# Splitting the merge's products between even and odd steps of a chunked delta-rule attention

## The chip, the cores and the metric

One core of a Trainium2 chip runs the whole program in one launch. The metric is the device time of an execution in microseconds, the median of three runs. Its engines are named as the profile does: PE is TensorE's matmuls, PEld its weight loads, DVE VectorE, ACT ScalarE, POOL GpSimd, SP SyncE, which issues the loads.

## The reference

A delta-rule attention of 4 batches x 8 heads, 768 tokens, head size 48, is followed by two MLP-like stages: a 2-D Fourier transform along tokens and channels with an MLP behind it, then a gated MLP whose gate is mixed along the tokens. The change touches only the attention:

```python
k_n = k / (np.linalg.norm(k, axis=-1, keepdims=True) + 1e-06)
state = np.zeros((B, H, D, D))
for t in range(S):
    kt, vt, bt = k_n[:, :, t], v[:, :, t], beta[:, :, t, None]
    y[:, :, t] = np.einsum('bhd,bhde->bhe', q[:, :, t], state)
    v_old = np.einsum('bhde,bhd->bhe', state, kt)
    state = state + bt[..., None] * np.einsum('bhd,bhe->bhde', kt, vt - v_old)
```

All is float32.

## The kernel before

**Chunks.** The 768 tokens are cut into 12 chunks of 64; with 4 batches that makes 48 units of work, which the code calls chunks and numbers bc = 0 to 47 in the order of a skewed list (`SEQ`). One chunk holds all 8 heads of its batch. In a chunk the recurrence becomes a triangular system of 64 x 64 per head: T, the inverse of a unit lower triangular matrix, is applied to the scaled keys and values, and the state is carried from chunk to chunk.

**Solver.** T is made for 8 chunks at a time (a block). VectorE inverts the two diagonal 32 x 32 squares of all of them together, at the end transposing them into `Tc` (line 346, two instructions); ScalarE takes the keys' norms (line 141). The solver is a generator. `Spread` advances it to a due share of its cost at fixed places of a step: `part(c1)` ahead of stage_d, `part(c2)` behind stage_a, `part(1)` at the end. A solver's steps are t = -3 to 2, 3 to 12, 13 to 20, 21 to 28 and 29 to 36 (`STARTS`).

**Loop.** `for t in range(-3, 48)` (line 631) does in each step, in this order: the scaling of chunk t + 2's values (`values`, on VectorE at line 488 for even chunks from 8 on, else on ScalarE), `part(c1)`, stage_d of chunk t (lines 533 and 534: output and new state `Sb`), stage_c of chunk t + 1 (line 513: keys times state; VectorE's `cw` at line 515) woven with stage_a of chunk t + 20 (line 220: Gram products), `part(c2)`, the diagonal of the next two chunks (`diag`), stage_b of chunk t + 2 (line 498: T times keys and values), in odd steps a `merge`, then the load of queries and `part(1)`. From t = 37 on steps are `light`: there is no solver. From t = 36 on the values of chunk t + 3 are scaled in the middle of step t (line 664), and the first products of the Fourier transform fill in behind stage_b. From then on `next(loads)` at the end of a step loads the transform's tables `sc` and `dc` (128 x 1281 and 97 x 386) and pieces of the weights, w.

**Merge.** The lower left square of T for chunks of a pair g8 comes from two rounds of products. The first: 16 products of 32 x 32 (line 467), the lower squares, `gas` times `Tc`, copied by ScalarE into `ZS` (line 471). The second: 16 products of 32 x 64 (line 469), the whole rows, `ZS` times `Tc`, copied into `TT` (line 474), which stage_b reads. Both write one PSUM bank (bankZ) at different partitions and rows. `merge(g8, first, second)` does the first for g8 and the second for g8 - 1. An odd step does both in one loop, product by product in turn, but for pairs whose first round stands at t % 8 = 5 by itself, where a new block begins.

**Loads of kv.** Keys and values of a chunk (192 KB) go into the space that the first round read (`gas`), so a load waits for the lower squares. It stands behind the merge of the odd step, two chunks at a time (lines 678 and 679).

**What sets the order.** Each engine takes its instructions in the order in which the code emits them: `chain()` at the end of each step ties every instruction to the one before it on its engine. SyncE's queue is filled in that order too.

Of the kernel before, what the change touches and what calls it, by code (L numbers as in the profile page):

```python
# [23 lines left out]
NBC = B * NC  # L24
# [42 lines left out]
class Kernel:  # L67
# [36 lines left out]
    def load(self, out, in_):  # L104
        return self.nc.sync.dma_start(out=out, in_=in_)
# [13 lines left out]
    def attention(self, cp, pg, pe, p, x, filler, after_solves):  # L119
# [115 lines left out]
        def mask_q(bc):  # L235

            out = gas[bc // 4 * 4, 4][:, bc % 4 : bc % 4 + 2, :, :C]
            first, second = (SEQ[i][1] < HALF for i in (bc, bc + 1))
            if first == second:
                m = mask_a(bc, C).unsqueeze(1)  # L240
            else:
                m = mk[:, : 4 * C].rearrange("p (a c) -> p a c", a=2)[:, :, :C]
                m = (m[:, ::-1] if first else m).unsqueeze(2)
            nc.vector.tensor_tensor(out=out, in0=out, in1=m.to_broadcast([128, 2, HP, C]), op=MUL)
# [202 lines left out]
        light = lambda t: t >= 8 * NB - 11  # L447

        def diag(g8):

            o = (g8 % 4) * 8
            for h, us in enumerate(up):
                (nc.vector.tensor_copy if light(2 * g8 - 3) else nc.scalar.copy)(
                    out=TT[g8 % NTT][us, :, C * h + 32 : C * h + C], in_=Tts[g8 // 4][us, o : o + 8]
                )

        def merge(g8, first, second):

            z0, z1 = zz[:, g8 % 2 * 256 : g8 % 2 * 256 + 256].rearrange("p (g n) -> p g n", g=8), zz.rearrange("p (g n) -> p g n", g=8)
            T0, o0 = (Tts[g8 // 4] if first else None), (g8 % 4) * 8  # L460
            T1, o1 = (Tts[(g8 - 1) // 4] if second else None), ((g8 - 1) % 4) * 8
            tt = TT[(g8 - 1) % NTT]
            for g in range(8):
                for h in range(2):
                    if first:
                        ga = gas[g8 * 2 + g // 4][:, g % 4]
                        nc.tensor.matmul(z0[lo[h], g], lhsT=ga[up[h], C : C + 32], rhs=T0[up[h], o0 + g], start=True, stop=True)
                    if second:
                        nc.tensor.matmul(z1[up[h], g], lhsT=T1[lo[h], o1 + g], rhs=ZS[(g8 - 1) % 2][lo[h], g], start=True, stop=True)  # L469
            if first:  # L470
                nc.scalar.mul(ZS[g8 % 2][:96, :, 32:], z0[:96], -1.0)
            if second:
                for h in range(2):
                    nc.scalar.copy(out=tt[lo[h], :, C * h : C * h + C], in_=z1[up[h]])


        def load_kv(bc):
            load(out=gas[bc][:, :, C:], in_=a["kv"][bc])

        def load_qt(bc):  # L480
            qts[bc] = p.tile([112, HP, 112], F32, name="qt", bufs=CF["qt"])
            load(out=qts[bc], in_=a["qt"][bc])

        def values(bc):
            kv = gas[bc][:, :, C:]
            if light(bc - 2) or bc >= 8 and bc % 2 == 0:
                n = n_all[:, bc * 4 : bc * 4 + 4].unsqueeze(2).to_broadcast([128, HP, D])
                nc.vector.tensor_tensor(out=kv[:, :, D:], in0=kv[:, :, D:], in1=n, op=MUL)  # L488
                return
            for hp in range(HP):  # L490
                nc.scalar.activation(kv[:, hp, D:], kv[:, hp, D:], AF.Copy, scale=n_all[:, bc * 4 + hp : bc * 4 + hp + 1])

        def stage_b(bc):
            kv = gas[bc][:, :, C:]
            tt, o = TT[(bc // 2) % NTT], (bc % 2) * 4
            pb = self.bank("pb", [128, HP, 2, D])
            for hp in range(HP):
                nc.tensor.matmul(pb[:, hp].rearrange("p t d -> p (t d)"), lhsT=tt[:, o + hp], rhs=kv[:, hp], start=True, stop=True)  # L498
            wu = WU[bc % NWU]
            nc.scalar.copy(out=wu, in_=pb.rearrange("p h t d -> p h (t d)"))  # L500
            st[bc] = [wu, None]

        def stage_c(bc):
            qt = qts.pop(bc)
            if SEQ[bc][1] == 0:
                return
            w = st[bc][0]
            cw = p.tile([112, HP, 112], F32, name="cw", bufs=2)
            pc = self.bank("pc", [128, HP, 112])
            for hp in range(HP):  # L510
                for h in hs:

                    nc.tensor.matmul(pc[h, hp], lhsT=w[h, hp, :C], rhs=gas[bc][h, hp, : C + D], start=True, stop=True)  # L513
                yield
            nc.vector.tensor_sub(cw, qt, pc[:112])  # L515
            st[bc][1] = cw
# [40 lines left out]
        for n in "kq":  # L557
            t = p.tile([128, 4, HP, GA], F32, name="gak", bufs=3).rearrange("p a b c -> p (a b c)")[:112, :2048]
# [62 lines left out]
        solver, c1, c2 = None, *CF["cuts"]  # L621
# [9 lines left out]
        for t in range(T0, NBC):  # L631
            if t in STARTS:
                if solver:
                    solver.finish()
                j, span, total = STARTS[t]
                solver, since = Spread(solve(j), total), t
            part = (lambda f: solver.upto(SECOND(t + f) if j == 1 else (t - since + f) / span)) if solver and not light(t) else (lambda f: None)
            if light(t) and solver:
                solver.finish()
                solver = None  # L640

            if 0 <= t + 2 < NBC and (not light(t) or (t + 2) % 8 == 0):
                values(t + 2)
            for bc in ahead.get(t, ()):
                mask_q(bc)
            part(c1)
            if t >= 0:
                stage_d(t)
                if SEQ[t][1] == NC - 1:
                    fill.extend(filler(SEQ[t][0]))  # L650
            new = t % 8 == 5 and t + 3 < NBC
            if new:

                merge((t + 3) // 2, True, False)
                load_kv(t + 3)
                load_kv(t + 4)
                diag((t + 3) // 2)
            corrected = stage_c(t + 1) if 0 <= t + 1 < NBC else iter(())
            if t + R + 2 < HEAD or HEAD <= t + R < NBC:
                stage_a(t + R + 2 * (t < 4), corrected)  # L660
            for _ in corrected:
                pass
            if light(t + 1) and t + 3 < NBC and (t + 3) % 8:
                values(t + 3)
            part(c2)
            odd = t % 2 and (t + 3) // 2 < NBC // 2
            if t == NBC - 12:
                solver.finish()
                loads, tail = after_solves()
            if t % 2 == 0 and t % 8 != 4 and t + 4 < NBC:  # L670
                diag((t + 4) // 2)
            if (odd or light(t + 1)) and 0 <= t + 2 < NBC:
                stage_b(t + 2)
            if odd:
                g = (t + 3) // 2
                merge(g + 1, (g + 1) % 4 > 0, True)
                if (t + 5) % 8 and t + 5 < NBC:
                    load_kv(t + 5)
                    load_kv(t + 6)
            if light(t + 1):  # L680

                for _ in range(CF["dfs"][t - (NBC - 12)]):
                    while fill and next(fill[0], 1) == 1:
                        fill.pop(0)
                for _ in range(CF["cvt"][t - (NBC - 12)]):
                    next(tail, None)
            elif not odd and 0 <= t + 2 < NBC:
                stage_b(t + 2)
            if 2 <= t + 4 < NBC:
                load_qt(t + 4)  # L690
            if t == -2:
                right(2)
                left(2)
            if t == -1:
                right(3)
            if t == 0:
                left(3)
            part(1)

            while late:  # L700
                out, m0, m1 = late.pop()
                nc.vector.tensor_tensor(out=out, in0=m0, in1=m1, op=MUL)
            self.chain()
            next(loads, None)
            if t >= NBC // 2:
                next(self.words, None)
            self.chain()
# [753 lines left out]
```

## Time and profile before

| | |
|---|---|
| Runs | 843.97, 844.51, 844.6 us; median 844.51 |
| Profiled execution | 842.8 us, span 841.0 us |
| TensorE (PE) | 807.8 us busy, 96%, 10291 matmuls |
| VectorE (DVE) | 599.6 us, 71% |
| ScalarE (ACT) | 408.9 us, 49% |
| GpSimd (POOL) | 7.6 us, 1% |
| Chain that ended last | PE 83%, DVE 11%, issue 2%, DMA 2% |
| kv loads | 48 issues, 192 KB, 3.8 us to landing |

The shares are means over stages that differ: the chain that ended last is TensorE's for most of the span, since the two MLPs behind the attention are TensorE's alone. The attention's loop is a quarter of the span. There the time of a step is read from the busy time of each engine in a stretch (windows), and from what its idle time waited for. The granted clock (PEclk) is a share of TensorE's 2.4 GHz; 0.50 is 1.2 GHz.

### The profile page before, as it was taken

The page shows a single profiled execution, that of the slowest core. Times are in us where ns is not written, and L with a number is a line of the kernel's source. Part 1 is how long each engine was busy: PE and PEld are TensorE (multiplying, and loading weights), DVE is VectorE, ACT ScalarE, POOL GpSimd, SP SyncE. Part 2 cuts the span into 40 slices and gives each one's busy share as a digit, 9 for nine tenths or more (in the row PEclk, how much of TensorE's full clock was granted, in tenths as well). Part 3 has the DMA queues.
Part 4 walks back from the last instruction along what each step waited for, and adds up shares of the span by engine and source line. Part 5 has one row for each costly group of instructions (what it writes and reads, how often), then busy time and mean ns, then how long its engine had stood idle before and what let it go on. Part 6 is the DMA issues. An engine that isn't in the chain of part 4 may idle for free.

```text
span 841.0 us, 24593 instructions
## 1 busy us (share of the span) xinstructions
PE 807.8 (96%) x10291; PEld 770.3 (92%) x10291; DVE 599.6 (71%) x1715; ACT 408.9 (49%) x1026; POOL 7.6 (1%) x60
## 2 busy tenths in 40 slices
PE   7898898889999999999999999999999999999998
PEld 7788787878988999899999999999899899899998
DVE  6988779999978995682935983345678477586663
ACT  3668868878665543232232551233452553543632
POOL 1000000000000000000000000000000000000000
PEclk9769979999999999999999999999999999999999
DMA  9634444456624200000114310112001101102001
GB/s 232 175 92 125 139 122 133 110 171 175 180 80 147 103 0 2 0 13 18 42 32 124 98 34 15 48 55 66 20 9 45 62 15 43 57 25 70 21 1 57
DMA packets 56417, 62.10 MB, mean 74 GB/s; under 512 B 31665, under 2 KB 48786, under 8 KB 56306
## 3 DMA queue, kind: packets, MB, share of 16 engines
q1 hardware_dynamic: 56162, 60.38, 24.6%
q8 instruction: 81, 1.33, 0.7%
q14 instruction: 30, 0.25, 0.1%
q10 hardware_dynamic: 144, 0.15, 0.1%
HBM read 48.12 MB, written 4.72 MB: 63 GB/s over the span
## 4 chain that ended last, share of the span: by engine, by line
PE 83%; DVE 11%; issue 2%; DMA 2%; ACT 1%; SPq 0%; ACTq 0%; DVEq 0%
PE bankX L946 17%; PE bankY L959 15%; PE bankX L1144 10%; PE bankX L1124 6%; PE bankX L1092 6%; PE bankY L1172 5%; PE bankY L498 4%; PE bankX L220 3%; PE bankY L533 2%; PE bankY L513 2%; PE bankV L959 2%; PE bankX L759 2%; PE bankY L534 2%; DVE cw L515 1%; PE bankZ L469 1%
## 5 line engine op out<-in xcount | busy, mean ns | idle before, releaser
L959 PE MATMUL bankY<-w,hx 128*128 128x384 f32 x756 | 147.2, 337 | 0.0
L946 PE MATMUL bankX<-uh,w 128*128 128x384 f32 x504 | 137.8, 340 | 0.7 <-DVE ul L868 0.7
L959 PEld LDWEIGHTS bankY<-w,hx 128*128 128x128 f32 x756 | 132.4, 188 | 0.5 <-issue 0.3
L951 DVE SCALAR_TENSOR_TENSOR hx<-bankX,hx 128x384 fp32r<-128x384 f32 x84 | 46.3, 552 | 74.4 <-ACT hx L950 71.9
L950 ACT ACTIVATE hx<-bankX 128x384 fp32r<-128x384 f32 x84 | 41.2, 490 | 109.6 <-PE bankX L946 105.2
L946 PEld LDWEIGHTS bankX<-uh,w 128*128 128x128 f32 x504 | 92.2, 188 | 1.2 <-DVE ul L868 0.9
L1144 PE MATMUL bankX<-w,A 128*128 128x384 f32 x504 | 88.8, 335 | 0.0
L1144 PEld LDWEIGHTS bankX<-w,A 128*128 128x128 f32 x504 | 87.6, 188 | 0.0
L946 PE MATMUL bankX<-ul,w 128*128 128x384 f32 x252 | 85.1, 338 | 0.0
L498 PE MATMUL bankY<-gak,TT 128*128 128x96 f32 x384 | 58.7, 299 | 5.3 <-DVE gak L488 1.9
L498 PEld LDWEIGHTS bankY<-gak,TT 128*128 128x128 f32 x384 | 50.5, 204 | 14.2 <-issue 2.8
L534 PE MATMUL bankY<-WU,gak 64*64 64x48 f32 x768 | 52.1, 231 | 0.0
L1124 PE MATMUL bankX<-xh,s 128*128 128x384 f32 x192 | 50.0, 338 | 0.0
L534 PE MATMUL bankY<-Sb,cw 48*64 48x48 f32 x704 | 47.5, 226 | 2.0 <-issue 2.0
L1133 ACT CAST u<-hx 128x384 fp32r<-128x384 f32 x32 | 15.8, 513 | 67.6 <-DVE hx L1131 67.6
L220 PE MATMUL bankX<-kq 48*64 48x128 f32 x640 | 48.0, 298 | 0.5 <-issue 0.5
L946 PEld LDWEIGHTS bankX<-ul,w 128*128 128x128 f32 x252 | 47.4, 188 | 0.0
L533 PE MATMUL bankY<-Sb,cw 48*48 48x48 f32 x640 | 38.8, 211 | 8.8 <-DVE cw L515 6.4
L513 PE MATMUL bankY<-gak,WU 64*64 64x112 f32 x704 | 46.0, 270 | 1.3 <-issue 1.3
L1092 PE MATMUL bankX<-s,xh 128*128 128x512 f32 x144 | 45.9, 395 | 0.0
L533 PE MATMUL bankY<-WU,gak 64*64 64x48 f32 x704 | 44.9, 232 | 0.6 <-ACT gak L200 0.6
L533 PEld LDWEIGHTS bankY<-WU,gak 64*64 64x64 f32 x704 | 37.5, 141 | 4.9 <-issue 1.0
(240 smaller groups left out, 1846.9 us busy)
## 6 DMA issues: line engine op xcount, KB each, us to landing
qt<-in_qt_dram SPq DMA_DIRECT2D x48, 196.0 KB, 3.4
gak<-in_kv_dram SPq DMA_DIRECT2D x48, 192.0 KB, 3.8
w<-in_w_dram SPq DMA_DIRECT2D x24, 384.0 KB, 5.6
kq<-in_kc_dram SPq DMA_DIRECT2D x20, 448.0 KB, 4.1
out_dram<-x SPq DMA_DIRECT2D x24, 192.0 KB, 1.9
x<-x SPq DMA_DIRECT2D x96, 36.0 KB, 1.9
s<-in_wi_dram SPq DMA_DIRECT2D x6, 512.0 KB, 4.3
un<-xh SPq DMA_DIRECT2D x80, 36.0 KB, 1.9
```

What stands on the lines that cost most here:

```text
L220: nc.tensor.matmul(pa[q, hp], lhsT=kq[r, hp, C:], rhs=kq[r, hp], start=True, stop=True)
L498: nc.tensor.matmul(pb[:, hp].rearrange("p t d -> p (t d)"), lhsT=tt[:, o + hp], rhs=kv[:, hp], start=True, stop=True)
L513: nc.tensor.matmul(pc[h, hp], lhsT=w[h, hp, :C], rhs=gas[bc][h, hp, : C + D], start=True, stop=True)
L533: nc.tensor.matmul(ps[C * i : C * i + n - C, hp], lhsT=k[:, C:n], rhs=u, start=not last, stop=end)
L534: nc.tensor.matmul(po[hs[1 - i], hp], lhsT=k[:, :C], rhs=u, start=not last, stop=end)
L946: nc.tensor.matmul(ph, lhsT=w1[f][i][:, c * 128 : c * 128 + 128], rhs=cur[k][:, c], start=(c + j == 0), stop=(c == 2 and j == 2))
L951: nc.vector.scalar_tensor_tensor(out=hl, in0=ph, scalar=0.0, in1=hh.bitcast(F32), op0=MAX, op1=SUB)
L959: nc.tensor.matmul(acc[t], lhsT=hx[i][:, t * 128 : t * 128 + 128], rhs=w2[e][k], start=(e == 0 and j == 0), stop=(e == 11 and j == 2),)
L1092: nc.tensor.matmul(pv, lhsT=xT[t][i][:, c, kk * 128 : kk * 128 + 128], rhs=wi[2 * c + 1][k], start=(c + j == 0), stop=(c == 2 and j == 2))
L1124: nc.tensor.matmul(pu, lhsT=wi[2 * c][i][:, f * 128 : f * 128 + 128], rhs=xT[hf][k][:, c], start=(c + j == 0), stop=(c == 2 and j == 2))
L1144: nc.tensor.matmul(acc, lhsT=A[:, m, o, i, kk], rhs=Bo[name, kk][:, k], start=(kk + j == 0), stop=(kk == 2 and j == 2))
L1172: nc.tensor.matmul(po, lhsT=a[:, :128], rhs=wo[f][k], start=(f + j == 0), stop=(f == last and j == 2))
```

## The change

The merge's two rounds part. An odd step does the second alone (`merge(g + 1, False, True)`); the first moves to the even step behind it, behind stage_b (in light steps behind the transform's products), for t % 8 other than 4. The loads of kv for two chunks move with it, so they are issued one step later. The values of the even chunks that VectorE scales (`sooner`: chunks 8 and up, not those of bc % 8 = 0, nor light ones) are scaled at the end of the odd step instead of the start of the next. And `part(c1)` is left out in a solver's last step (t = 12, 20, 28 and 36), so what it would have emitted there comes with `part(c2)` and `part(1)`.

```diff
--- before.py
+++ after.py
@@ -490,6 +490,9 @@
             for hp in range(HP):
                 nc.scalar.activation(kv[:, hp, D:], kv[:, hp, D:], AF.Copy, scale=n_all[:, bc * 4 + hp : bc * 4 + hp + 1])
 
+        def sooner(bc):
+            return 8 <= bc < NBC and bc % 8 in (2, 4, 6) and not light(bc - 2)
+
         def stage_b(bc):
             kv = gas[bc][:, :, C:]
             tt, o = TT[(bc // 2) % NTT], (bc % 2) * 4
@@ -639,11 +642,12 @@
                 solver.finish()
                 solver = None
 
-            if 0 <= t + 2 < NBC and (not light(t) or (t + 2) % 8 == 0):
+            if 0 <= t + 2 < NBC and (not light(t) or (t + 2) % 8 == 0) and not sooner(t + 2):
                 values(t + 2)
             for bc in ahead.get(t, ()):
                 mask_q(bc)
-            part(c1)
+            if t - since < span - 1:
+                part(c1)
             if t >= 0:
                 stage_d(t)
                 if SEQ[t][1] == NC - 1:
@@ -673,10 +677,7 @@
                 stage_b(t + 2)
             if odd:
                 g = (t + 3) // 2
-                merge(g + 1, (g + 1) % 4 > 0, True)
-                if (t + 5) % 8 and t + 5 < NBC:
-                    load_kv(t + 5)
-                    load_kv(t + 6)
+                merge(g + 1, False, True)
             if light(t + 1):
 
                 for _ in range(CF["dfs"][t - (NBC - 12)]):
@@ -686,6 +687,10 @@
                     next(tail, None)
             elif not odd and 0 <= t + 2 < NBC:
                 stage_b(t + 2)
+            if t % 2 == 0 and t % 8 != 4 and t + 4 < NBC:
+                merge((t + 4) // 2, True, False)
+                load_kv(t + 4)
+                load_kv(t + 5)
             if 2 <= t + 4 < NBC:
                 load_qt(t + 4)
             if t == -2:
@@ -700,6 +705,8 @@
             while late:
                 out, m0, m1 = late.pop()
                 nc.vector.tensor_tensor(out=out, in0=m0, in1=m1, op=MUL)
+            if sooner(t + 3):
+                values(t + 3)
             self.chain()
             next(loads, None)
             if t >= NBC // 2:
```

TensorE at steps 22 and 23 before: L498 (stage_b) ends the even step, L533 and L534 are stage_d of the next; `WU`, `TT`, `ZS` and `Tc` are the tiles named above.

```order
L513 MATMUL bankY<-gak,WU_92 64x112 x2
L498 MATMUL bankY<-gak,TT_89 128x96 x4
L533 MATMUL bankY<-WU_92,gak 64x48
L534 MATMUL bankY<-WU_92,gak 64x48
...
L498 MATMUL bankY<-gak,TT_89 128x96 x4
L467 MATMUL bankZ<-Tc,gak 32x32
L469 MATMUL bankZ<-ZS_85,Tc 32x64
L467 MATMUL bankZ<-Tc,gak 32x32
```

The same places in the changed kernel, where stage_b is L501 and stage_d L536 and L537:

```order
L516 MATMUL bankY<-gak,WU_92 64x112 x2
L501 MATMUL bankY<-gak,TT_89 128x96 x4
L467 MATMUL bankZ<-Tc,gak 32x32 x16
L536 MATMUL bankY<-WU_92,gak 64x48
...
L501 MATMUL bankY<-gak,TT_89 128x96 x4
L469 MATMUL bankZ<-ZS_85,Tc 32x64 x16
L536 MATMUL bankY<-WU_91,gak 64x48
```

The 16 lower squares of the odd step's mixture now stand between the even step's stage_b and the next stage_d.

VectorE at step 12 before: the values of chunk 14 (L488; `n_all` are the norms), the solver's two transposes into `Tc`, then `cw` of chunk 13, between masks of the Gram products.

```order
L702 TENSOR_TENSOR gak<-bankX,mk 128x4x64
L488 TENSOR_TENSOR gak<-gak,n_all 128x4x48
L346 STREAM_TRANSPOSE Tc<-Ts 128x16x32 x2
L515 TENSOR_TENSOR cw<-qt,bankY 112x448
L702 TENSOR_TENSOR gak<-bankX,mk 128x4x64
```

And in the changed kernel:

```order
L707 TENSOR_TENSOR gak<-bankX,mk 128x4x64
L488 TENSOR_TENSOR gak<-gak,n_all 128x4x48
L518 TENSOR_TENSOR cw<-qt,bankY 112x448
L346 STREAM_TRANSPOSE Tc<-Ts 128x16x32 x2
L707 TENSOR_TENSOR gak<-bankX,mk 128x4x64
```

`cw` has come ahead of both transposes; the values stand where they stood.

SyncE's queue at steps 36 to 39 before: the tables `sc` and `dc`, the kv of chunks 40 to 43 (four) between them, and weight pieces w.

```order
L105 DMA s_4902<-in_sc_dram 128x1281
L105 DMA gak<-in_kv_dram 128x4x96 x4
L105 DMA qt<-in_qt_dram 112x448
L105 DMA s_4903<-in_dc_dram 97x386
L105 DMA w_3_5056<-in_w_dram 128x768
L105 DMA qt<-in_qt_dram 112x448
L105 DMA w_5_5130<-in_w_dram 128x768
L105 DMA gak<-in_kv_dram 128x4x96 x2
```

And in the changed kernel:

```order
L105 DMA s_4902<-in_sc_dram 128x1281
L105 DMA gak<-in_kv_dram 128x4x96 x2
L105 DMA qt<-in_qt_dram 112x448
L105 DMA s_4903<-in_dc_dram 97x386
L105 DMA w_3_5037<-in_w_dram 128x768
L105 DMA gak<-in_kv_dram 128x4x96 x2
L105 DMA qt<-in_qt_dram 112x448
```

The kv of chunks 42 and 43, the last two of the four, have come behind `dc` and a weight piece.

## Rows read from the trace of the kernel before

**Rows 1.** Windows: stretch, us; busy us (count) PE, PEld, DVE, ACT, POOL; clock; DMA; GB/s.

```profile
56.00:111.50 55.50, 49.13 (x1616) 43.80 (x1615) 43.70 (x136) 44.86 (x140) 1.70 (x19) 0.96 0.45 128
111.50:122.00 10.50, 10.26 (x234) 9.44 (x238) 6.30 (x34) 5.45 (x17) 0.16 (x1) 0.51 0.38 105
122.00:207.00 85.00, 75.45 (x2543) 67.29 (x2535) 81.93 (x306) 69.11 (x205) 1.85 (x20) 1.00 0.53 147
207.00:262.00 55.00, 52.20 (x1418) 47.32 (x1413) 46.17 (x124) 34.38 (x91) 0.00 (x0) 0.97 0.38 110
```

**Rows 2.** TensorE's waits, 124 to 207 us: line, waited for: us, times, longest.

```profile
PE bankY L533 <- DVE cw L515: 3.0, 5, 1.0
...
PE bankY L498 <- DVE gak L488: 1.9, 2, 1.2
```

**Rows 3.** TensorE's waits, 56 to 111.5 us.

```profile
PE bankY L533 <- ACT gak L200: 0.6, 1, 0.6
```

**Rows 4.** Windows: the loop's start, and the stretch ahead of the fall.

```profile
36.00:57.00 21.00, 20.85 (x456) 18.61 (x453) 20.66 (x80) 13.99 (x44) 0.00 (x0) 0.50 0.44 123
...
108.14:111.55 3.41, 1.93 (x40) 1.50 (x30) 3.38 (x7) 2.42 (x9) 0.77 (x9) 1.00 0.19 66
```

**Rows 5.** Windows, bankZ alone (no POOL column): squares, whole rows, both mixed.

```profile
76.00:78.00 2.00, 0.69 (x32) 0.58 (x32) 0.00 (x0) 0.00 (x0) 1.00 0.03 8
...
144.00:146.00 2.00, 1.08 (x32) 0.92 (x32) 0.00 (x0) 0.18 (x1) 1.00 0.24 53
...
153.00:155.50 2.50, 1.10 (x64) 0.94 (x64) 0.00 (x0) 0.65 (x2) 1.00 0.50 119
```

**Rows 6.** The chain near 113 us: start us, us, what (count).

```profile
113.49 0.99 PE bankZ L467 x32
```

**Rows 7.** Timeline, steps 8 and 9: start us, us, engine line op [idle before <-releaser].

```profile
93.05 1.13 PE L498 MATMUL bankY<-gak,TT 128*128 128x96 f32 x8
...
98.62 0.35 DVE L488 TENSOR_TENSOR gak<-gak,n_all 128x192 f32<-128x192 f32 x1
```

**Rows 8.** DMA issues, 216 to 219.3 us: count, KB each, us to landing.

```profile
gak<-in_kv_dram SPq DMA_DIRECT2D x2, 192.0 KB, 4.0
```

**Rows 9.** Timeline, steps 38 to 41, stage_b, values, stage_d.

```profile
221.60 1.24 PE L498 MATMUL bankY<-gak,TT 128*128 128x96 f32 x8
...
226.06 0.35 DVE L488 TENSOR_TENSOR gak<-gak,n_all 128x192 f32<-128x192 f32 x1
...
232.08 0.25 PE L533 MATMUL bankY<-WU,gak 64*64 64x48 f32 x1
```

**Rows 10.** SyncE's timeline (its DMA queue), 216 to 231 us.

```profile
216.58 4.57 SPq L105 DMA_DIRECT2D gak<-in_kv_dram  x4
...
221.86 0.33 SPq L105 DMA_DIRECT2D s<-in_dc_dram  x1
...
226.26 1.24 SPq L105 DMA_DIRECT2D gak<-in_kv_dram  x2
...
230.96 0.31 SPq L105 DMA_DIRECT2D qt<-in_qt_dram  x1
```

**Rows 11.** DMA issues, 225 to 228 us.

```profile
gak<-in_kv_dram SPq DMA_DIRECT2D x2, 192.0 KB, 8.1
```

**Rows 12.** SyncE's waits, 229 to 236 us.

```profile
SPq L105 <- DMA s<-in_dc_dram: 0.5, 1, 0.5
```

**Rows 13.** Timeline, step 12, 108.8 to 111.7 us.

```profile
108.81 0.23 ACT L141 ACTIVATE n<-sq 128x32 f32<-128x32 f32 x1 [0.87 <-DVE sq L262]
...
109.03 0.35 DVE L488 TENSOR_TENSOR gak<-gak,n_all 128x192 f32<-128x192 f32 x1
...
109.29 1.95 DVE L346 STREAM_TRANSPOSE Tc<-Ts 128x512 f32<-128x512 f32 x2
...
109.63 1.10 PE L498 MATMUL bankY<-gak,TT 128*128 128x96 f32 x8 [0.92 <-ACT Sb L542]
...
111.10 0.59 DVE L515 TENSOR_TENSOR cw<-qt,bankY 112x448 f32<-112x448 f32 x1
```

## Prediction

> **What bounds the kernel now.** I read the stretches of the attention stage first, since the change touches only the loop over steps t = -3 to 47, which fills about 36 to 262 us of the 841.0 us span. From 56 to 111.5 us TensorE, VectorE and ScalarE are busy for 49.1, 43.8 and 44.9 of 55.5 us (in the profile's windows PE, DVE and ACT): TensorE leads and no engine is full. From 122 to 207 us VectorE is busy for 81.9 of 85 us and TensorE for 75.5; from 207 us on TensorE for 52.2 of 55 [rows 1]. So more work for TensorE should cost most before 111 us and after 207 us, and least between. Next the waits: from 124 to 207 us TensorE loses 3.0 us at line 533 to VectorE's cw (5 waits) and 1.9 us at line 498 to the scaled values [rows 2]. Before 111.5 us one wait of 0.6 us, for ScalarE, is of that kind [rows 3]. Third, the granted clock: full before, 0.51 from 111.5 to 122 us [rows 1], and what came ahead of that fall was a stretch in which TensorE was busy for 1.93 of 3.41 us [rows 4]. The loop's first 21 us run at 0.50 as well [rows 4].
>
> **The change part by part.**
>
> *The split merge.* The odd step's merge had 16 products of the lower squares (line 467), each between two of the 16 of the whole rows (line 469). Both together take 1.10 us; the whole rows alone took 1.08, the squares alone 0.69, by the windows around one merge of each kind [rows 5]: in the mixture they hide each other. So the odd step keeps its length but for 0.02 us, and each even step with squares of its own grows by 0.69 - 0.02, say 0.65 us; at the low clock squares alone take 0.99 [rows 6], say 1.0. Eighteen merges are split, at the even t from -2 to 42 without those of t % 8 = 4.
> - t = -2, 0, 2: TensorE has no wait to fill there (busy for 20.85 of 21 us [rows 4]); the clock is low for the first and about the last: 1.0 + 0.65 + 1.0 = 2.6 us.
> - t = 6, 8, 10: the squares of 6 go right ahead of step 7's stage_d, whose wait of 0.6 us [rows 3] they fill: nothing. 8 and 10 have no such wait: 1.3 us.
> - t = 14 to 34, nine merges, 5.9 us of TensorE: VectorE sets the pace [rows 1]. Four of the five cw waits stand in a stage_d right behind an even step, where the squares now go; 3.0 us in five, and at most 0.65 of each is filled, so some 2.3 us cost nothing. For the other 3.6 the bounds are 0 (VectorE has other work meanwhile) and 3.6 (stage_c, and with it cw, comes as much later); VectorE, 96% busy, speaks for the lower half, and I take 1.5.
> - t = 38, 40, 42: those of 38 come ahead of a wait, and of 42 I expect the same: nothing (0.65 each if not). Those of 40 go into the last term.
>
> *The loads of kv.* They still wait for the squares, and so are issued one step later. Up to t = 34 this just costs nothing. The shortest way is that of chunk 12: stage_b of step 8 ends at 93.05 + 1.13 = 94.2 us, its values are scaled at 98.62 [rows 7]; half the squares (0.3) and a landing of 4.0 us [rows 8] make 98.5. The end of the loop is different. There even chunks' values are scaled in the middle of odd steps (line 664): chunk 42's at 226.06 us; stage_b of step 38, behind which its load now goes, ends at 221.60 + 1.24 = 222.8 us [rows 9]. With 0.3 and 4.0 that is 227.1, 1.0 us late. But the queue ahead of it changes too. Before, kv of 42 and 43 left among the four that begin at 216.58 us, ahead of the table dc (221.86) [rows 10]; now dc and one piece of the weights go first. What was queued behind dc landed late: the kv issued at 226.26 us [rows 10] took 8.1 us [rows 11] instead of 4.0 [rows 8], to 234.4. SyncE waited for dc until 230.9 us [rows 10, 12], 9 us behind its issue. With two kv loads fewer ahead of it dc may leave some 2 us sooner and land at 228.8; by the same distance (234.4 - 230.9 = 3.5 us with two weight pieces between, here one) chunk 42's kv lands between 230 and 232, and I take 230.4. VectorE then stands for 230.4 - 226.3 = 4.1 us, and it takes its work in order: behind these values stand the sums that feed the DFT, and then cw of step 41. TensorE has to wait for them in its DFT products and starts step 41's stage_d, at 232.08 us before [rows 9], 4.1 us later, and 0.65 more for the squares of 40. From there to the loop's end TensorE is nearly full [rows 1], so nothing gives this back: 4.7 us. The bounds are 0.6 (kv is in time) and 6.5 (it lands at 232).
>
> The Trainium skill, "DMA: Bandwidth & Descriptors", section "Why a DMA increments its semaphore by 16 and not by 1", says that a DMA is spread over the largest number of engines, up to 16, that divides its slowest dimension. By that rule dc, of 97 rows, would sit on one engine, and only the part of kv on that engine would be held up; the late landings behind dc agree, though no view here shows single engines. Without it, by the landing of 4.0 us alone, the sum would be some 3 us less.
>
> *Values at the end of the odd step.* On VectorE nothing was issued between the end of a step and the start of the next, so the instruction stands where it stood. Cost 0.
>
> *part(c1) left out in a solver's last step.* It moves cw. At t = 20 and 28 cw goes ahead of the first of two transposes of Tc; what follows needs both, and their end doesn't move but by cw's 0.59 us, under VectorE's full load: 0. At t = 12 it goes ahead of both. There stage_b waited 0.92 us until 109.63 us for ScalarE's copy of Sb, and ScalarE had stood 0.87 us at line 141; then stage_d waited for cw, which stood behind two transposes of 1.95 us, until 111.7 us [rows 13]. Now line 141 comes behind ScalarE's copies, stage_b can start with the values (109.4), and cw is done by 110.0 us. Both waits go; the next is that of step 13's squares for Tc, 0.6 us later than before, at 111.9 instead of 113.4 (their start [rows 6]): 1.5 us gained. These waits are what stood ahead of the fall of the clock [rows 4]. Without them I expect no fall. What the 10.5 us at half speed can give back is bounded by VectorE, busy for 6.30 of them [rows 1]: at most 4.2 us, the 1.5 included. I take -4.2 without the fall; with it, -1.5.
>
> **Sum**, against the profiled execution's own 842.8 us (the span of 841.0 and 1.8 around it): 2.6 + 1.3 + 1.5 - 4.2 + 4.7 = +5.9, so 848.7. The median of the runs, 844.51, is 1.7 above it, so I forecast 850.4.
>
> The Trainium skill, "TensorEngine Tiling (Array Packing)", section "Key Properties", has the engine drain whenever its tiling mode changes, which speaks against splitting a group. The rows for squares and whole rows alone [rows 5] hold such a change already. By the rule as by the rows the sum stays.
>
> **Rivals.**
> 1. The clock falls at 111 us anyway. For it: step 13's squares and a wait for Tc are still there, at little work for TensorE. Against: two waits go. Then 2.6 + 1.3 + 1.5 - 1.5 + 4.7 = +8.6: 853.1.
> 2. Chunk 42's kv lands in time, since dc is the smaller part of what fills the queues there. Against: dc's 9 us. Then 4.7 becomes 0.6 and the sum +1.8: 846.3.
> 3. Faster: TensorE's extra products are hidden in every even step, because the waits behind them end on ScalarE and VectorE, whose order doesn't change. For it: VectorE's 81.9 of 85 us, and no engine full before 111 us. Against: TensorE leads there. Its place is the even steps from 8 to 34; the squares cost nothing, kv is in time, the clock doesn't fall: -4.2 + 0.6 = -3.6, 840.9. It decides if stage_d of the odd steps starts no later, behind the end of the step's chain on VectorE, than before.
> That the change doesn't do what it says holds for the values alone (above).
>
> **How the numbers follow.** Forecast 0.42, rival 1 0.20, rival 2 0.20, rival 3 0.18. A measurement of this kernel tells 0.2% from no change, which is 1.7 us: from 842.8 to 846.2 is no change. The forecast and rival 1 lie above that; rival 2 lies at its upper edge, and I count 0.05 of it as slower and 0.15 as the same; rival 3 is faster but for 0.02. Faster 0.16, same 0.17, slower 0.67. The terms' bounds (0 to 3.6, 0.6 to 6.5, -1.5 to -4.2) give the forecast its own range of 846 to 854, and rival 1 up to 856; with rival 2 and a part of rival 3 the whole range is 842 to 856.
>
> **What would show it.** In the profile after: line 467 alone with some 0.69 us at the end of even steps; less waiting at the stage_d behind them; no clock at half speed near 111 us; VectorE waiting about 4 us at line 488 for kv near the loop's end. It would be wrong if that wait is under 1 us, or if the even steps before 111 us are no longer than before.

## The result and the profile after

The changed kernel took 854.27 us (median of 8 runs, 847.76 to 856.51), the kernel before 845.61 us beside it (8 runs, 843.97 to 847.76): a ratio of 1.0089, with a 95% interval of 1.0063 to 1.0114 (the two medians alone give 1.0102). The change is slower, where 850.4 us had been forecast. Ratios and their intervals, here and below, leave out executions of more than 1.5% above the fastest of the same kernel; medians and ranges are over all. The profiled execution took 855.76 us. Its page begins so (span; busy time of each engine; granted clock in 40 slices):

```profile
span 854.0 us, 24588 instructions
...
PE 822.1 (96%) x10291; PEld 782.6 (92%) x10291; DVE 599.4 (70%) x1715; ACT 408.4 (48%) x1026; POOL 7.6 (1%) x60
...
PEclk9769999999959999999999999999999999999999
```

The work is the same; TensorE is busy for 14.3 us more. The slices place most of that: one 5 in the twelfth slice, near the loop's end, which the kernel before did not have. The windows of the same columns as [rows 1] show the stretches:

```profile
111.50:122.00 10.50, 9.01 (x284) 7.82 (x280) 10.16 (x39) 7.63 (x24) 0.93 (x10) 1.00 0.48 133
122.00:207.00 85.00, 79.35 (x2532) 70.90 (x2525) 80.54 (x304) 68.58 (x205) 1.86 (x20) 1.00 0.53 146
...
230.40:233.70 3.30, 1.46 (x10) 1.31 (x10) 2.35 (x5) 1.42 (x4) 0.00 (x0) 0.96 0.49 143
233.70:253.00 19.30, 19.30 (x216) 17.53 (x214) 6.89 (x16) 6.10 (x15) 0.00 (x0) 0.50 0.16 44
```

The low clock that [rows 1] had from 111.5 to 122 us is gone: 1.00 there, and 284 matmuls instead of 234. From 122 to 207 us TensorE works 3.9 us more and VectorE 1.4 us less. And from 233.7 to 253 us TensorE now runs at half speed, behind 3.3 us in which it was busy for 1.46.

What stands ahead of that, in the timeline of VectorE, TensorE and SyncE's queue at steps 38 to 40 (start, us, instruction, and in brackets the idle time before it and what ended it):

```profile
231.28 0.36 DVE L488 TENSOR_TENSOR gak<-gak,n_all 128x192 f32<-128x192 f32 x1 [3.95 <-DMA gak<-in_kv_dram]
```

```profile
231.90 1.10 PE L501 MATMUL bankY<-gak,TT 128*128 128x96 f32 x8 [1.54 <-DVE gak L488]
233.35 0.53 PE L760 MATMUL bankX<-s,s 128*97 128x65 f32 x2 [0.35 <-DVE s L748]
```

```profile
220.27 0.33 SPq L105 DMA_DIRECT2D s<-in_dc_dram  x1
220.65 0.69 SPq L105 DMA_DIRECT2D w<-in_w_dram  x1
224.57 1.22 SPq L105 DMA_DIRECT2D gak<-in_kv_dram  x2
```

Chunk 42's values waited 3.95 us for kv, which now leaves at 224.57 us behind dc (before: 216.58, ahead of it [rows 10]) and took 6.8 us to land (median of the two). Behind them TensorE stood for 1.54 us in stage_b and 0.35 us at the transform's products.

The squares alone in an even step, in a window of bankZ as in [rows 5], take what they were priced at:

```profile
84.50:86.00 1.50, 0.69 (x32) 0.58 (x32) 0.00 (x0) 0.08 (x1) 1.00 0.04 7
```

### The profile page after: what moved, and what is told of

It reads as the page before. It is cut to its first block, busy times and chain, and to the rows that moved or that the text cites. A ratio compares the mean times of both kernels' runs of the same rounds, so it can differ in the third digit from the quotient of the medians.

```text
span 854.0 us, 24588 instructions
## 1 busy us (share of the span) xinstructions
PE 822.1 (96%) x10291; PEld 782.6 (92%) x10291; DVE 599.4 (70%) x1715; ACT 408.4 (48%) x1026; POOL 7.6 (1%) x60
## 4 chain that ended last, share of the span: by engine, by line
PE 84%; DVE 9%; issue 2%; DMA 2%; ACT 1%; SPq 0%; ACTq 0%; DVEq 0%
PE bankX L953 17%; PE bankY L966 15%; PE bankX L1151 10%; PE bankX L1131 6%; PE bankX L1099 6%; PE bankY L1179 5%; PE bankY L501 4%; PE bankX L220 3%; PE bankX L766 2%; PE bankZ L469 2%; PE bankY L516 2%; PE bankV L966 2%; PE bankY L536 2%; PE bankY L537 2%; PE bankZ L467 1%
## 5 line engine op out<-in xcount | busy, mean ns | idle before, releaser
L501 PE MATMUL bankY<-gak,TT 128*128 128x96 f32 x384 | 57.7, 296 | 5.7 <-DVE gak L488 2.2
L501 PEld LDWEIGHTS bankY<-gak,TT 128*128 128x128 f32 x384 | 49.7, 202 | 14.4 <-issue 4.2
L537 PE MATMUL bankY<-WU,gak 64*64 64x48 f32 x768 | 50.3, 227 | 0.1
L537 PE MATMUL bankY<-Sb,cw 48*64 48x48 f32 x704 | 45.4, 222 | 0.9 <-issue 0.9
L536 PE MATMUL bankY<-WU,gak 64*64 64x48 f32 x704 | 43.1, 226 | 1.5 <-ACT WU L503 0.8
L518 DVE TENSOR_TENSOR cw<-qt,bankY 112x448 f32<-112x448 f32 x44 | 27.0, 614 | 21.3 <-PE bankX L220 10.9
L536 PEld LDWEIGHTS bankY<-WU,gak 64*64 64x64 f32 x704 | 36.7, 137 | 5.0 <-issue 1.9
```

The lines of the kernel that those rows point to most:

```text
L536: nc.tensor.matmul(ps[C * i : C * i + n - C, hp], lhsT=k[:, C:n], rhs=u, start=not last, stop=end)
L537: nc.tensor.matmul(po[hs[1 - i], hp], lhsT=k[:, :C], rhs=u, start=not last, stop=end)
```

## The experiments

Two theories stood at first. A: the loss lies at the loop's end, where kv is late because dc stands ahead of it, and the low clock follows from that wait. B: the low clock comes somewhere anyway. Since the executions of one kernel differ by several us here (the kernel before from 839.4 to 855.0 us in the 35 runs of one series), most of what follows rests on the profiles: on the time from the start of one stage_b to that of another, read from the traces. Steps -2 to 6 are the time from stage_b of step -2 to that of step 6, and so on; a star marks a part in which the clock was low (at the start every kernel has it low until 57 to 62 us, which is not marked; the two profiles in which it stayed low until 66 and 67 us are).

| Kernel | -2 to 6 | 6 to 12 | 12 to 14 | 14 to 35 | 37 to 39 | 39 to 42 |
|---|---|---|---|---|---|---|
| before | 41.37* | 26.92 | 12.75* | 87.75 | 6.88 | 16.51 |
| before, again | 39.99 | 30.86* | 8.51 | 90.14* | 6.80 | 17.06 |
| before, cw first | 40.31* | 31.55* | 7.72 | 88.00 | 7.17 | 16.51 |
| before, cw first, second series | 40.27* | 28.53 | 8.70 | 94.47* | 7.30 | 21.90* |
| before, dc ahead | 41.89* | 34.14* | 8.57 | 89.08 | 13.86* | 16.31 |
| split to 10 | 40.52 | 30.70* | 9.35 | 88.02 | 6.91 | 17.06 |
| split 14 to 34, cw first | 40.53 | 26.84 | 7.44 | 89.77* | 7.31 | 19.70* |
| changed | 40.38 | 30.26 | 8.57 | 88.94 | 7.61 | 28.62* |
| changed, again | 42.58* | 31.20* | 12.27* | 95.22* | 7.36 | 21.76* |
| changed, end joined | 40.08 | 30.22 | 9.20 | 88.67 | 6.74 | 16.41 |
| changed, dc a step later | 40.01 | 31.37* | 7.44 | 88.25 | 9.67* | 17.46* |
| changed, dc in two | 40.23 | 30.40 | 8.53 | 93.95* | 7.36 | 17.10 |
| changed, cw behind | 40.12 | 28.90 | 12.08* | 91.10* | 7.36 | 20.45 |
| changed, filled | 40.73 | 30.92 | 7.97 | 88.70 | 7.77 | 20.58 |

**The end joined.** In the changed kernel, from step 37 on:

```diff
-                merge(g + 1, False, True)
+                merge(g + 1, t >= 37 and (g + 1) % 4 > 0, True)
+                if t >= 37 and (t + 5) % 8 and t + 5 < NBC:
+                    load_kv(t + 5)
+                    load_kv(t + 6)
...
-            if t % 2 == 0 and t % 8 != 4 and t + 4 < NBC:
+            if t % 2 == 0 and t % 8 != 4 and t + 4 < 42:
```

> The changed kernel, but from step 37 on the merge has both rounds in the odd step again, with the loads of kv there (chunks 42 to 47). Theory A: the 12 us lost after step 38 (VectorE's wait of 4.0 us for chunk 42's kv, and the low clock of some 19 us that follows it) both hang on kv being late; then neither is there, and steps 38 to 45 take what they took in the kernel before: a profiled span near 842 us (854.0 - 12.4), ratio to the kernel before about 1.001. Rival B: the low clock comes anyway near the loop's end (it has only moved there from 111 us): the wait goes, the low clock stays, a span near 850.

The span was 842.6 us, steps 39 to 42 took 16.41 us, and the clock stayed up from 218 to 252 us. The ratio to the kernel before was 1.0046 (1.0015 to 1.0077). So what is lost at the end hangs on the moved squares and loads there; half of the slowdown or so remains.

**dc a step later.** In the loads of the loop's end, dc goes out with the second weight piece instead of the first:

```diff
-                self.load(out=self.dc, in_=a["dc"])
                 for i in range(CF["ahead"]):
+                    if i == 1:
+                        self.load(out=self.dc, in_=a["dc"])
```

> The changed kernel, with the table dc loaded one step later (end of step 38, behind the kv of chunks 42 and 43, which stay behind the squares of step 38). Theory A says that it is dc ahead in the queue that holds kv up: kv of 42 lands some 4 to 5 us behind its issue, at about 229, the wait is under 1 us, no low clock follows, span 842 to 843. Rival C, that kv is late because it is issued a step later whatever stands ahead: the wait stays above 2.5 us, and the span above 850.

VectorE's waits and kv's landing (x2, KB each, us to landing) at the same place, in two views:

```profile
DVE gak L488 <- DMA gak<-in_kv_dram: 0.3, 1, 0.3
```

```profile
gak<-in_kv_dram SPq DMA_DIRECT2D x2, 192.0 KB, 3.8
```

kv is still issued behind the squares of step 38, and lands in 3.8 us: C falls, what stands ahead decides. The span was 844.9 us (a low clock of 3.4 us at 225 us, behind a stand of 0.7 us of another kind), the ratio 1.0032 (1.0001 to 1.0063).

**dc in two.** The same bytes at the same place in the queue, by rows:

```diff
-                self.load(out=self.dc, in_=a["dc"])
+                self.load(out=self.dc[:96], in_=a["dc"][:96])
+                self.load(out=self.dc[96:], in_=a["dc"][96:])
```

> The changed kernel, with dc (97 rows) loaded by two DMAs, of 96 rows and of 1 row, at the same place. If dc holds kv up because its 97 rows are not spread over the engines, it lands within 5 us of its issue instead of 9, kv of chunk 42 at about 228.5, VectorE's wait is near 1 us and the span 842 to 844. If it is the bytes in the queue (sc, dc, weights, kv), splitting changes nothing: the wait stays near 4 us and the span near 854.

dc's 96 rows (144.8 KB) landed in 4.0 us, and the kv behind them:

```profile
s<-in_dc_dram SPq DMA_DIRECT2D x1, 144.8 KB, 4.0
```

```profile
gak<-in_kv_dram SPq DMA_DIRECT2D x2, 192.0 KB, 3.9
```

```profile
DVE gak L488 <- DMA gak<-in_kv_dram: 0.9, 1, 0.9
```

Not the bytes but the shape, one load of 97 rows, held kv up. Issuing kv a step later costs little by itself: VectorE's wait is 0.9 us here, with dc's bytes still ahead, and was 0.3 us with dc behind. Steps 39 to 42 took 17.10 us. The span, 850.2, misses the 842 to 844 expected: the clock was low from 178 to 182 and from 198 to 209 us, where nothing had been changed. The ratio was 1.0026 (0.9994 to 1.0058).

**dc ahead, in the kernel before.** The fault made there: dc at the end of step 36, ahead of the kv of chunks 40 to 43.

```diff
                 self.load(out=self.sc, in_=a["sc"])
-                yield
                 self.load(out=self.dc, in_=a["dc"])
+                yield
```

> The kernel before with dc loaded one step earlier, at the end of step 36, so that it stands ahead of the kv of chunks 40 to 43 (issued at 216.6 us before). Theory A (what is queued behind dc lands late): the kv of chunk 40 lands 3 to 5 us later than before, VectorE waits 3 to 5 us for it near 222 us (0.4 us at most before), and TensorE's steps 38 to 40 come as much later. Rival: dc does not matter, kv lands 4 us behind its issue and the steps stay as they were.

The waits of VectorE and TensorE at steps 38 to 40, and the clock there (windows):

```profile
DVE gak L488 <- DMA gak<-in_kv_dram: 5.0, 1, 5.0
```

```profile
PE bankY L498 <- DVE gak L488: 4.7, 1, 4.7
```

```profile
232.00:239.00 7.00, 4.83 (x88) 4.67 (x88) 4.20 (x15) 1.28 (x4) 0.00 (x0) 0.51 0.68 206
```

The kv of chunk 40 took 9.3 us to land:

```profile
gak<-in_kv_dram SPq DMA_DIRECT2D x1, 192.0 KB, 9.3
```

In this one execution, one line moved brings the wait into a kernel that did not have it, and steps 37 to 39 from 6.88 to 13.86 us, low clock included.

**The changed kernel again.** No edit.

> The changed kernel once more, beside the others. The wait of some 4 us for chunk 42's kv is in the queue's order and comes again, at the same step. If the low clock behind it is a consequence of that wait, it comes again in the profile or in most executions, and the median stays some 0.7 to 1.1% above the kernel before; if it was chance, the span is near 845.

The ratio was 1.0059 (1.0009 to 1.0108), the median 853.55 us, beside 846.69 for the kernel before: 1.0081 by the medians. In the profiled execution (863.36 us) VectorE's wait for kv was there, and the clock was low behind it, but briefly; elsewhere it was low where the first profile had it full:

```profile
DVE gak L488 <- DMA gak<-in_kv_dram: 3.8, 1, 3.8
```

```profile
122.00:136.00 14.00, 14.00 (x255) 12.59 (x249) 7.90 (x46) 8.11 (x24) 0.07 (x1) 0.51 0.42 112
204.00:214.00 10.00, 10.00 (x163) 8.95 (x163) 4.11 (x18) 4.10 (x12) 0.00 (x0) 0.50 0.46 139
248.00:252.00 4.00, 4.00 (x25) 3.75 (x27) 3.36 (x8) 0.48 (x1) 0.00 (x0) 0.57 0.01 4
```

The wait belongs to the kernel; how long the clock stays low behind it, if at all, differs from execution to execution.

**The wait filled.** In the changed kernel, ahead of stage_b in step 40:

```diff
+            if t == 40:
+                wb = self.bank("pf", [128, 256])
+                for _ in range(7):
+                    nc.tensor.matmul(wb, lhsT=self.idn, rhs=mk[:, :256], start=True, stop=True)
```

> The changed kernel with seven products of 128 x 256 whose result nobody reads, put in front of stage_b of step 40, where TensorE stood 1.5 us for chunk 42's values. Theory A: TensorE's standing is what precedes the low clock of 233 to 254 us; filled, VectorE still waits 4 us for kv and step 41 is still 4 us late, but the clock stays up: a span near 845 (854.0 - 9). Rival E: the low clock comes all the same, since kv is late: span near 854, or the products themselves delay stage_b and add up to 1.6 us.

VectorE waited 4.7 us and the clock stayed at 1.00 from 232 to 256 us; steps 39 to 42 took 20.58 us. But the median was 855.23 us, the ratio 1.0106 (1.0063 to 1.0148): no gain over the changed kernel, where 9 us had been expected. The products ran for 3.3 us, longer than the 1.5 us they were to fill. And the next kernel, unfilled, stayed up as well. So the profile that looked like a proof is none.

**cw behind the transposes again.** In the changed kernel, without its condition on part(c1):

```diff
-            if t - since < span - 1:
-                part(c1)
+            part(c1)
```

> The changed kernel with part(c1) kept in a solver's last step (cw behind the transposes of Tc again). Theory A: the low clock ahead of step 13 is due to the two waits there; they come back, and with them 10 us at half speed near 111 us, 4 us more than the changed kernel from step 12 to 14 (11 us instead of 8.6). Rival D: the low clock there comes by chance in one execution or another; steps 12 to 14 then lose 0.6 to 1.5 us and no more.

Both waits of step 12 were back (0.4 and 0.8 us) and the clock fell behind them, from 115 to 129 us; at the loop's end VectorE waited 4.2 us for kv, TensorE 2.1 us, and the clock did not fall:

```profile
115.00:129.00 14.00, 14.00 (x254) 12.63 (x250) 8.18 (x47) 8.29 (x24) 0.15 (x1) 0.51 0.44 116
232.00:256.00 24.00, 21.30 (x435) 19.27 (x432) 15.79 (x38) 13.08 (x35) 0.00 (x0) 1.00 0.27 77
```

Theory A's sign, but the ratio, 1.0078 (1.0036 to 1.0120), can't be told from the changed kernel's. Whether the fall near step 12 belongs to those waits needed the next run.

**The kernel before again.** No edit, one execution.

> The kernel before once more, one look. If the low clock of 111 to 122 us belongs to its order of work (the two waits at step 12), it is there again, and steps 12 to 14 take 17.8 us again. If where the clock falls is chance, it falls elsewhere or not at all in the loop, and steps 12 to 14 take some 13.6 us, as in the run with dc ahead, whose order is the same up to step 36; the span then lies anywhere between 838 and 853.

TensorE's waits at step 12, and the clock of the stretch:

```profile
PE bankY L498 <- ACT Sb L542: 1.1, 1, 1.1
PE bankY L533 <- DVE cw L515: 0.7, 1, 0.7
```

```profile
111.50:122.00 10.50, 8.53 (x281) 7.41 (x273) 9.45 (x39) 7.95 (x24) 0.93 (x10) 1.00 0.40 101
```

The same waits as in [rows 13], and no fall; steps 12 to 14 took 8.51 us instead of 12.75. (The expectation counts three steps; from stage_b of step 12 to that of step 15 it is 12.69 us instead of 15.93.) The kernel with dc ahead, whose order is the same up to there, had both waits (0.9 and 0.7 us), no fall, and 8.57 us. So of four profiles with both waits two show the fall, the first of the kernel before and cw behind, and two don't: the waits are not enough for it.

**cw first, in the kernel before.** The condition on part(c1) alone; run in two series.

```diff
-            part(c1)
+            if t - since < span - 1:
+                part(c1)
```

> The kernel before, with one line of the change alone: part(c1) left out in a solver's last step, so that cw goes ahead of the transposes of Tc. Theory A: this alone takes away the low clock of 111 to 122 us, worth 4.2 us, so a span near 837 and a ratio near 0.995. Rival D: the split of the squares is needed as well (the joined merges leave TensorE less to do there), the clock falls as before, and the gain is 0 to 1.5 us.

> The kernel before with part(c1) left out in a solver's last step, as once already, to tell whether it or the split at steps 14 to 34 made the last version faster. If cw ahead of the transposes is the gain: ratio 0.995 to 0.998, as with the split. If it is the split (or chance): 0.999 to 1.001, and steps 12 to 14 take some 13 us (13.7 in the kernel before where the clock stayed up).

The ratios were 0.9995 (0.9963 to 1.0027) and 0.9965 (0.9934 to 0.9995), the medians 844.00 and 843.78 us. The first lies with D, the second nearer to A; at the same clock neither is clear of no change (see the end of the next section). In the first profile steps 12 to 14 took 7.72 us; the wait at stage_b was still there (1.0 us, for line 141 now).

**Split from 14 to 34, with cw first.** In the kernel before, the squares and their kv loads go to the even step under a condition on t:

```diff
-                merge(g + 1, (g + 1) % 4 > 0, True)
-                if (t + 5) % 8 and t + 5 < NBC:
+                apart = 14 <= t + 1 <= 34
+                merge(g + 1, (g + 1) % 4 > 0 and not apart, True)
+                if (t + 5) % 8 and t + 5 < NBC and not apart:
...
+            if t % 2 == 0 and t % 8 != 4 and 14 <= t <= 34:
+                merge((t + 4) // 2, True, False)
+                load_kv(t + 4)
+                load_kv(t + 5)
```

> The kernel before with the squares split off (and their kv loads behind them) only at even steps 14 to 34, and part(c1) left out in a solver's last step; the loop's start and end as before. Theory A: VectorE sets the pace there, so the nine splits cost 0 to 1.5 us, nothing at the loop's end is late, and the ratio is 0.998 to 1.002 against the kernel before. Rival F: the split products cost their whole 5.9 us: 1.007.

The median was 844.05 us, the ratio 0.9962 (0.9932 to 0.9993). The interval lies below 1. But these executions also had a higher mean clock than those of the kernel before beside them (0.977 and 0.972), and at the same clock nothing clear of the scatter is left (see the end of the next section). Nor can it be told from cw first alone in its second series. So no gain is shown for the split itself, and no cost either: F falls.

**Split to 10.** The same edit with `-2 <= t + 1 <= 10` and no condition on part(c1).

> The kernel before with the squares split off only at even steps -2 to 10. Theory A: TensorE leads there, five or six splits cost 2.6 + 1.3 = 3.9 us, ratio 1.003 to 1.005. Rival G (the squares hide behind ScalarE and VectorE there too): below 1.001.

The ratio was 1.0027 (0.9989 to 1.0066), which holds all of A's range as well as G's. The table says more; its reading rests on some waits. First TensorE's stands near step 2, in the kernel before again and in the changed kernel; "issue" says that the profile shows no releaser:

```profile
66.36 0.20 PE L533 MATMUL bankY<-Sb,cw 48*48 48x48 f32 x1 [1.52 <-issue]
```

```profile
64.75 0.35 PE L501 MATMUL bankY<-gak,TT 128*128 128x96 f32 x1 [0.71 <-issue]
```

Then stage_d of step 7 in the kernel before and in the changed kernel, and the changed kernel's waits for cw from 124 to 207 us (before: [rows 2]):

```profile
84.42 0.26 PE L533 MATMUL bankY<-WU,gak 64*64 64x48 f32 x2 [0.58 <-ACT gak L200]
```

```profile
86.13 0.26 PE L536 MATMUL bankY<-WU,gak 64*64 64x48 f32 x2 [0.79 <-ACT WU L503]
```

```profile
PE bankY L536 <- DVE cw L518: 0.4, 1, 0.4
```

## Why the prediction was right, and where its terms were not

The forecast ratio, 850.4 / 844.51 = 1.0070, lies in the measured interval, and the place and mechanism of the largest term were those forecast. But rival 1's ratio, 853.1 / 844.51 = 1.0102, lies there too, so the time alone doesn't tell the two apart, and that the sum came out is in part luck: three of its terms were wrong. (The forecast's own range is also too narrow: the terms' bounds, added up, give 844.8 to 857.0 us, not 846 to 854.) The terms, from parts of the table without a star:

- **The loop's end, forecast +4.7, measured +4.3.** VectorE was to wait 4.1 us (counted from 226.3 us, where [rows 9] have 226.06) and waited 3.95; kv was to land at 230.4 us, and the values started at 231.28. Steps 39 to 42 take 16.3 to 17.1 us with kv in time and 20.5 with kv late (3.8 more), steps 37 to 39 some 0.5 more. Dc as the cause was shown from both sides: by its shape, by its place, and in the kernel before. The rule of the Trainium skill, "DMA: Bandwidth & Descriptors", "Why a DMA increments its semaphore by 16 and not by 1", fits: 97 rows held the queue up, 96 and 1 did not. Rival 2 (kv in time) falls.
- **The squares at -2, 0 and 2, forecast +2.6, measured about 0.** Split kernels took 40.0 to 40.7 us up to step 6, the unsplit 40.0 and 40.5. The squares did cost time: from stage_b of step -2 to that of 0 the split kernels took 14.6 us or more, the unsplit 13.9, and from 2 to 4 8.1 us or more, the unsplit 7.6. From 0 to 2 they gained it back (mean 10.1 us against 11.4): the unsplit kernels stood 1.5 us ahead of stage_d of step 2, without a releaser, and the split ones didn't. The prediction found "no wait to fill there" in a window that ends at 57 us, ahead of that stand (2.07 us at 65.9 us in its own trace). So the term is hidden by a stand that it did not see, and which moved.
- **Those at 6, 8 and 10, forecast +1.3, measured +2.7 or so.** Split 28.9 to 30.9 us (mean 30.1), unsplit 26.8, 26.9 and 28.5, so that the size is rough. Steps 6 to 8 took no longer (9.97 to 10.38 us, unsplit 9.87 to 10.45), as forecast, though not because the squares of 6 fill the wait of step 7: in the changed kernel its stage_d waited as long behind them (0.79 us, 0.58 before), now for ScalarE's copy of WU. The loss is in steps 8 to 10: 9.6 to 11.2 us against 7.6, 8.2 and 9.8. There, too, TensorE's stands without a releaser take part, 1.0 to 2.6 us in the split kernels and 0, 0.6 and 2.0 in the unsplit. Without them it is 8.6 to 8.8 us against 7.6 to 7.8, so 1.0 where 0.65 was forecast for the squares of 8.
- **14 to 34, forecast +1.5, measured +0.4.** Split 88.3 to 88.9 us, unsplit 87.8 to 89.1. The two ranges overlap. The waits for cw at stage_d, of which 2.3 us were to be filled, fell from 3.0 us in five [rows 2] to 0.4 us in one. So VectorE sets the pace, and what rival 3 said for the whole loop holds here, but not at the loop's end or before step 12.
- **The clock at 111 us, forecast -4.2, measured -0.6.** This is the step that failed as a mechanism: two waits stood ahead of the fall, and "without them I expect no fall". The waits stood there in three more traces, in two of them with no fall behind; and the changed kernel's second profile had a fall there (122 to 136 us) without the wait for cw, behind stands of 0.92 and 1.15 us. So these waits are neither enough for the fall nor needed for it. Nor did both waits go: stage_b's stood on in five of nine profiles with cw first (0.9 to 1.0 us, for line 141). cw first makes steps 12 to 14 about 0.6 us shorter (7.4 to 9.2 us, mean 8.2, against 8.5 to 9.4 in three profiles, mean 8.8). The rest was one execution's low clock, which the median of many holds in other places. The Trainium skill, "TensorE: Matmul & The Clock Gate", "Part 1: The HAM clock gate", says of the slow start that it differs from run to run of one kernel; the two profiles of the kernel before show the same of a fall inside the loop (111 to 122 us in one; 102 to 106 and 160 to 164 us in the other). Rival 1 took the fall for the kernel's too, but its price for this term, -1.5, was the nearer one.

The sum of these, 4.3 + 0 + 2.7 + 0.4 - 0.6 = +6.8 us, compares with 7.5 us by the first ratio (0.0089 x 845.61; interval 5.3 to 9.6) and 5.0 by the second (0.0059 x 846.69); by the medians it is 8.7 and 6.9 us. The errors of three terms made up for each other: -4.2 was too much gain, 2.6 too much loss, and 1.3 too little. Of the profiled executions' difference, 13.0 us, some 8 are the low clock at 234 us, which was not forecast and is not the change's every time: two kernels with the same wait did not have it. The record speaks for its coming more often with the wait: beside the changed kernel again, the three kernels with the wait had a mean clock of 0.970 over 32 executions and the kernel before 0.975 over 27 (difference 0.001 to 0.008), while end joined, dc a step later and dc in two had 0.974, as the kernel before beside them.

The clock can also be taken out. Over the 102 executions of the kernel before that stood beside the other runs, 0.01 more of mean clock goes with 6.3 us less (each series against its own mean), and what is left scatters by 1.7 us. By this estimate, at the same clock, the changed kernel again is 5.3 us longer than the kernel before (4.5 to 6.1), cw behind 4.8 and filled 5.9; end joined, dc a step later and dc in two 2.5, 2.3 and 2.0 (give or take 0.9 to 1.4); split to 10 1.4 (0.2 to 2.5). Cw first (-0.6 and -1.0) and split 14 to 34 with cw first (-0.5) can't be told from no change. So of these 5.3 us some 3 hang on dc ahead of kv, fewer than the table's 4.3, and about 1.4 on the squares up to step 10; what the executions lose beyond 5.3 us goes with the clock.

## What to carry to other kernels

Before a load is moved by a step, look at what the same queue then carries ahead of it: a small table of 97 rows held a load up by some 3 us, and splitting it into 96 and 1 took that away. Don't count a low clock in one profile as the price of the wait ahead of it: take a second profile of the same kernel first. And look for stands that show no releaser before a difference of a microsecond is put down to a cause: when the order of work changed, they came, went and moved by as much as the products that were counted.

## What the runs showed of the hardware

Stretches at 1.2 GHz came in all but one of the profiles at different places of the loop, 3 to 20 us long, each during or behind a stand of TensorE of 0.4 to 4.7 us; but many such stands had none behind them. The longest stands of that kind often show no releaser ("issue"). One in the changed kernel, and the DMA queues just ahead of it (packets, MB, share of 16 engines; window 101.5 to 102.8 us):

```profile
104.24 0.31 PE L516 MATMUL bankY<-gak,WU 64*64 64x112 f32 x2 [2.06 <-issue]
```

```profile
q8 instruction: 1, 0.02, 5.6%
```

No load of instructions had been under way for nearly 5 us before that window, while the loads of the program took 89% of the engines' time. All 69 stands of more than 0.6 us without a releaser, between 57 and 262 us of the 14 traces, ended 1.2 to 1.7 us behind the end of a 16 KB load of that instruction queue, which come some 4 to 7 us apart. That TensorE stands there for its instructions is inferred from this, and so is that other loads hold them up; neither was tried.
